# One attention batch moved beside chunk 1's first layer, and both layers of the feed-forward part taken in turn from there on

**Chip, cores, metric.** One core of one Trainium2 chip. The time is device microseconds of an execution; "span" is the length of the profiled execution. "Before" was run again with every group of experiments, on the same chip as these, and its median went from 357.4 to 360.3 us. So kernels are compared by their ratio to the kernel before in the same rounds, not by their microseconds across groups.

## The reference

Sliding-window attention (window of 64 keys) over 8 batches of 8 heads, 576 positions, 64 features; its output feeds two matrix products with `h - tanh(h)` between them.

```python
scores = scale * np.matmul(q, k.transpose(0, 1, 3, 2))
mask = (rel >= 0) & (rel < window)          # rel = row - column, window = 64
attn = softmax(np.where(mask, scores, -1e9))
x = np.matmul(attn, v)                      # -> [4608 tokens, 512]
h = x @ w_in                                # [4608, 2048]   "first layer"
out = (h - np.tanh(h)) @ w_out              # [4608, 512]    "second layer"
```

## The kernel before: what the argument touches

The program is one list of **slots**. A slot holds at most one layer product, of four matmuls of 512 columns. Tokens are in 9 chunks of 512, attention is in 32 head pairs `g` (four per batch, `b = g // 4`). `at(h, fn, ...)` hangs other work on slot `h`; in the traces each engine runs its own instructions in this program order, so a slot is a place in each engine's queue and not a time. PE multiplies matrices, DVE and ACT work on elements, POOL casts and issues loads, SP issues the other transfers (DMA).

```python
NR, NPT = 2, 4                                   # buffers of q/k, of probabilities
v_pool = ctx.enter_context(tc.tile_pool(name="v", bufs=1))
vb = const.tile([PV, EV, H, D + 1], BF16, ...)   # a batch's values, cast: ONE buffer
vw = [const.tile([128, NJ, H, D + 1], BF16, ...) for i in range(2)]   # its 9 windows

def pace(h):             # holds POOL's queue until the last first-layer product before slot h is done
    c, m = [OPS[i][1:] for i in range(h) if OPS.get(i, "-")[0] == "h"][-1]
    nc.gpsimd.tensor_copy(tick, gT[c][0:1, m, 0:1])

# chain of a batch's values: load (POOL's DMA queue) -> cast_v into vb -> windows_v (SP's DMA queue, vb -> vw) -> pv (PE)
# x of a batch (b >= 3): norm (DVE) -> x_dma: transposing DMAs on SP's queue -> first-layer products
...
for m in range(M):                               # M = 16 products per chunk and layer
    OPS[2 * m] = "h", 0, m                       # "h": first layer, "y": second layer
    OPS[32 + m] = "y", 0, m
    OPS[48 + m] = "h", 1, m
    OPS[64 + m] = "y", 1, m
    OPS[80 + m] = "h", 2, m
    for c in range(3, NC):                       # from chunk 3 on both layers in turn
        OPS[32 * c + 2 * m] = "h", c, m
        OPS[32 * c + 2 * m + 1] = "y", c - 1, m
...
at(46, lambda: [cast_v(2, pr, V) for pr in range(NP)])        # V: DVE
at(47, lambda: [windows_v(2, j, Y) for j in range(NJ)])       # Y: SP's queue
# batches 2 and 3: a table of slots per pair, from 48 to 91; batch 3's x_dma at 92
```

The softmax here doesn't subtract the row's maximum and nothing guards it: scores larger than these inputs give would overflow.

## Time and profile before

| | before |
|---|---|
| median of 4 runs | 360.31 us (356.45 to 361.85) |
| span of the profiled run | 358.4 us |
| PE busy | 321.5 us, 90% |
| slot 48 / 64 / 96 starts (us) | 68.8 / 88.6 / 140.5 |

The slot times are read from the trace: PE's layer products stand in it in program order, so the start of the first of each four is the start of its slot. The profile's lines are shown and read in the prediction.

### The profile page before, as it was taken

How to read it: one execution, taken by the hardware profiler on the slowest of the kernel's cores; microseconds unless marked ns; L12 is line 12 of the kernel's file. 1: busy time of each engine (PE TensorE's matmuls, PEld its weight loads, DVE VectorE, ACT ScalarE, POOL GpSimd, SP SyncE). 2: the span in 40 equal slices, each digit the busy share in tenths (PEclk: the TensorE clock that was granted, in tenths of full speed). 3: DMA queues.
4: the chain of work that ended last, by engine and by line, in shares of the span. 5: the costliest groups of instructions: out<-in, count | busy, mean ns of one | idle time of the engine just before them, and what ended most of it. 6: DMA issues, size and time to landing. Idle time of an engine off the chain costs nothing.

```text
span 358.4 us, 6075 instructions
## 1 busy us (share of the span) xinstructions
PE 321.5 (90%) x2346; PEld 177.1 (49%) x2346; DVE 207.2 (58%) x344; ACT 182.9 (51%) x332; POOL 98.4 (27%) x148
## 2 busy tenths in 40 slices
PE   6789998699787986778879999999999999999995
PEld 2554454455454553435445555555555444444442
DVE  4566765677954885346657767665666334433300
ACT  3536545288554764516636566655554444444421
POOL 8821090033731610517063445801000000000000
PEclk9559999699999999969999999999999999999999
DMA  8999999839189206991856989489930410010012
GB/s 162 167 199 215 182 160 207 148 49 183 29 119 247 60 1 118 134 170 45 157 119 112 203 145 174 125 140 202 203 108 29 98 59 29 31 59 29 31 67 79
DMA packets 54653, 42.96 MB, mean 120 GB/s; under 512 B 23232, under 2 KB 48320, under 8 KB 54624
## 3 DMA queue, kind: packets, MB, share of 16 engines
q0 software_dynamic: 20816, 18.73, 34.5%
q1 hardware_dynamic: 33456, 23.42, 28.0%
q10 hardware_dynamic: 352, 0.43, 0.5%
q8 instruction: 18, 0.29, 0.3%
q14 instruction: 11, 0.09, 0.1%
HBM read 36.70 MB, written 11.21 MB: 134 GB/s over the span
## 4 chain that ended last, share of the span: by engine, by line
PE 62%; DMA 17%; DVE 11%; ACT 4%; POOL 3%; issue 2%; POOLq 0%; ACTq 0%
PE ps L417 28%; PE ps L393 26%; DMA vall<-in_v_dram 11%; DMA vw<-vb 5%; DVE gT L405 3%; DVE xs L357 3%; PE ps L346 3%; PE ps L334 3%; DVE qt L86 2%; PE ps L267 2%; DMA qall<-in_q_dram 2%; ACT qt L84 1%; ACT th L398 1%; ACT pt L336 1%; PE ps L363 1%
## 5 line engine op out<-in xcount | busy, mean ns | idle before, releaser
L393 PE MATMUL ps<-xT,wi 128*128 128x512 bf16 x576 | 146.2, 383 | 6.6 <-DVE gT L405 6.5
L417 PE MATMUL ps<-w_out_sb,gT 128*128 128x512 bf16 x576 | 145.7, 382 | 0.5 <-ACT ysb L422 0.5
L405 DVE TENSOR_TENSOR gT<-ps,th 128x512 bf16<-128x512 f32 x144 | 98.3, 690 | 80.8 <-ACT th L398 79.1
L398 ACT ACTIVATE th<-ps 128x512 f32<-128x512 f32 x144 | 85.6, 598 | 85.5 <-PE ps L393 81.4
L393 PEld LDWEIGHTS <-wi 128*128 128x128 bf16 x576 | 62.1, 114 | 55.6 <-issue 9.8
L417 PEld LDWEIGHTS <-gT 128*128 128x128 bf16 x576 | 53.6, 98 | 53.9 <-issue 1.8
L336 ACT ACTIVATE pt<-ps 128x384 bf16<-128x384 f32 x72 | 35.1, 488 | 30.8 <-PE ps L334 30.6
L357 DVE TENSOR_TENSOR xs<-ps,rc 64x576 bf16<-64x576 f32 x48 | 36.2, 755 | 1.2
L422 ACT ACTIVATE ysb<-ps 128x512 f32<-128x512 f32 x36 | 21.5, 596 | 19.1 <-PE ps L417 19.1
L346 PE MATMUL ps<-vw,pt 128*128 128x130 bf16 x216 | 22.3, 220 | 7.7 <-DMA vw<-vb 5.8
L86 POOL COPY vb<-vall 72x1024 bf16<-72x1024 bf16 x20 | 20.9, 1067 | 28.9 <-DMA vall<-in_v_dram 17.8
L346 PEld LDWEIGHTS <-pt 128*128 128x128 bf16 x216 | 16.9, 98 | 19.1 <-issue 6.6
L334 PE MATMUL ps<-qt,kt 128*128 128x128 bf16 x216 | 24.2, 222 | 1.3 <-ACT pt L336 1.2
L334 PEld LDWEIGHTS <-kt 128*128 128x128 bf16 x216 | 17.1, 99 | 14.2 <-issue 5.3
L86 DVE COPY qt<-ps 64x576 bf16<-64x576 bf16 x20 | 15.2, 760 | 13.8 <-ACT qt L84 13.7
L86 POOL COPY qb<-qall 96x768 bf16<-96x768 bf16 x16 | 13.2, 825 | 30.2 <-DMA qall<-in_q_dram 30.2
L340 DVE TENSOR_TENSOR pt<-pt,ps 128x1152 bf16<-128x1152 bf16 x24 | 17.9, 747 | 0.2
L86 POOL COPY kb<-kall 96x768 bf16<-96x768 bf16 x20 | 16.5, 828 | 0.0
L84 ACT ACTIVATE kt<-ps 128x576 bf16<-128x576 bf16 x20 | 13.0, 650 | 4.7 <-PE ps L267 4.6
L353 DVE RECIPROCAL rc<-ps 128x9 f32<-128x9 f32 x24 | 5.2, 215 | 16.8 <-PE ps L346 16.7
L84 ACT ACTIVATE qt<-ps 64x576 bf16<-64x576 bf16 x20 | 12.7, 637 | 3.1 <-PE ps L267 3.1
L309 ACT ACTIVATE pt<-ps 128x640 bf16<-128x640 f32 (+1 forms) x16 | 10.0, 649 | 5.7 <-PE ps L306 5.6
(74 smaller groups left out, 189.0 us busy)
## 6 DMA issues: line engine op xcount, KB each, us to landing
out_dram<-ysb SPq DMA_DIRECT2D x36, 256.0 KB
vw<-vb SPq DMA_DIRECT2D x48, 130.0 KB
vall<-in_v_dram POOLq DMA_DIRECT2D x7, 576.0 KB, 13.7
kall<-in_k_dram POOLq DMA_DIRECT2D x5, 576.0 KB, 7.1
qall<-in_q_dram POOLq DMA_DIRECT2D x5, 576.0 KB, 9.4
wi<-in_moe_w_in_dram POOLq DMA_DIRECT2D x2, 1024.0 KB, 12.8
w_out_sb<-in_moe_w_out_dram POOLq DMA_DIRECT2D x2, 1024.0 KB, 20.9
kall<-in_k_dram POOLq DMA_DIRECT2D x11, 144.0 KB, 13.8
```

The lines of the kernel that those rows point to most:

```text
L84: nc.scalar.activation(o, i, ACT.Copy)
L86: eng.tensor_copy(o, i)
L334: nc.tensor.matmul(sp[:, i, :], kT[g % NR][:, 64 * j:64 * j + 128], qT[g % NR][:, :, 64 * j:64 * j + 64], start=True, stop=True)
L336: nc.scalar.activation(PT[g % NPT][:, 3 * grp:3 * grp + 3, :], sp, ACT.Exp, scale=scale)
L340: nc.vector.tensor_tensor(p, p, mask.unsqueeze(1).to_broadcast([128, 2 * NJ, 64]), ALU.mult)
L346: nc.tensor.matmul(ps[:, 5 + grp, 130 * i:130 * i + 130], PT[g % NPT][:, j, :], vw[b % 2][:, j, 2 * pr:2 * pr + 2, :], start=True, stop=True)
L357: nc.vector.tensor_tensor(xo[r, :, :, pr, :], ov[r, :, :, h, 0:D], rc[r].to_broadcast([64, 3, 3, 64]), ALU.mult)
L393: nc.tensor.matmul(hp, w_in_tile(ki, m), chunk_tile(c)[:, :, ki % 2, 64 * (ki // 2):64 * (ki // 2) + 64], start=(ki == 0), stop=(ki == 3))
L398: nc.scalar.activation(th, hp, ACT.Tanh)
L405: nc.vector.tensor_tensor(gT[c][:, m, :], hp, th, ALU.subtract)
L417: nc.tensor.matmul(yp, gT[c][:, m, s * 128:(s + 1) * 128], w_out_sb[:, m, :], start=(m == 0), stop=(m == M - 1))
L422: nc.scalar.activation(ysb, ps[:, yp_bank(c, s), :], ACT.Copy)
```

## The change

Its intent: first-layer products alone make PE wait for tanh and subtraction, so after chunk 1's first layer both layers alternate. For that, chunk 2's input (batch 2) must be ready by slot 66 and not 80. So batch 2 goes entirely beside chunk 1's first layer (slots 48 to 65), its mask added by a product on PE ahead of the scores, its value products in column tiles; batches 3 to 5 move with it, and batch 3's loads lose the `pace` that held them. Cut to its core (left out: the layers' PSUM banks, batch 6, and the slots of some casts):

```diff
-        OPS[64 + m] = "y", 1, m
-        OPS[80 + m] = "h", 2, m
+        OPS[66 + 2 * m if m < 15 else 95] = "h", 2, m
+        OPS[63 + 2 * m if m > 1 else 64 + m] = "y", 1, m
...
-    at(35, load_v_all, 2)
     for g in 8, 9, 10, 11:
         at(35, load, g, "k", G)
         at(35, load, g, "q", G)
+        if g == 8:
+            at(35, load_v_all, 2)
...
-    at(46, lambda: [cast_v(2, pr, V) for pr in range(NP)])
-    at(47, lambda: [windows_v(2, j, Y) for j in range(NJ)])
-    at(54, pace, 54)
-    at(54, load_all, 3, "k")   # q at 55, v at 56; values cast at 67-70, windows at 71
+    at(47, cast_pair, 8, V)
+    at(48, cast_pair, 9, G)
+    at(49, lambda: [cast_v(2, pr, V) for pr in range(NP)])
+    at(50, lambda: [windows_v(2, j, Y) for j in range(NJ)])
+    at(52, load_all, 3, "k")   # q at 52, v at 53
+    for i, (g, p) in enumerate(((8, 58), (9, 59), (10, 61), (11, 63))):
+        at(48 + 3 * i, tr, g, "q", 3, A, V)
+        at(49 + 3 * i, tr, g, "k", 3, A)
+        for j in range(3):
+            at(50 + 3 * i + j, hidden_scores, g, j, 4 + (3 * i + j) % 2)   # mask product + scores
+        at(p, tile_pv, g, (6, 7))
...
-    LOADS = {4: (77, 78, 79), 5: (97, 98, 99), 6: (128, 130, 113)}      # slots of k, q, v
+    LOADS = {4: (63, 64, 72), 5: (96, 99, 102), 6: (124, 128, 114)}
+        if b == 3:
+            a = (62, 67, 72, 76)[pr]        # a: slot of the pair's first transpose
+            cv, ky = 63 + pr, 67            # cv: slots of the value casts, ky: first windows
-        if b == 4: a = (89, 95, 101, 108)[pr]; cv, ky = 91 + pr, 95
+        elif b == 4: a = (80, 87, 95, 102)[pr]; cv, ky = 77 + 3 * pr, 88
-        elif b == 5: a = 110 + 7 * pr; cv, ky = 108 + pr, 112
+        elif b == 5: cv, ky = 107 + 2 * pr, 114
             at(ky + j // 2, windows_v, b, j, Y)      # unchanged: nine windows over five slots
```

## The prediction

> **What bounds the kernel now.** I read the page first, then the table of busy time in stretches of 10 us, then the waits of PE, then PE's order of instructions from 56 to 220 us, then the DMA packets. The table by stretches tells where there is anything to win:
>
> ```profile
> core 0: us, PE busy (x) PEld busy (x) DVE busy (x) ACT busy (x) POOL busy (x), PEclk, DMA share, GB/s
> ...
> 60.00:70.00 10.00, 5.70 (x101) 4.11 (x100) 6.50 (x16) 4.10 (x9) 0.64 (x1) 0.69 0.92 161
> ...
> 130.00:140.00 10.00, 5.83 (x44) 3.53 (x44) 8.41 (x14) 5.07 (x9) 0.00 (x0) 1.00 0.35 62
> ...
> 150.00:160.00 10.00, 6.03 (x23) 2.73 (x22) 3.72 (x6) 2.46 (x6) 1.59 (x2) 0.66 1.07 191
> ...
> 210.00:220.00 10.00, 10.00 (x78) 5.87 (x77) 7.12 (x12) 6.14 (x13) 5.81 (x9) 1.00 1.01 176
> ```
>
> From 210 us to the end PE is full: there both layers alternate with one head pair of attention per eight slots. All that can be won lies between 60 and 210 us, where PE's busy sums to 125.0 of 150 us. Each stall also hides some 0.17 us (a matmul's record is 0.38 us, its pitch 0.216), so about 40 stalls add 6 to 7 us; two cold stretches (PEclk 0.69 and 0.66) cost about 4. In all about 35 us are lost there, and that is the ceiling. PE's order of instructions names the causes:
>
> ```profile
> 60.74 0.44 PE L306 MATMUL ps<-qs,kt 64*128 64x64 bf16 x18
> 62.34 0.51 PE L322 MATMUL ps<-vw,pt 128*64 128x65 bf16 x20 [1.17 <-ACT pt L309]
> 64.81 1.14 PE L363 MATMUL ps<-ident,xs 128*128 128x128 bf16 x9 [1.96 <-DVE xs L328]
> ...
> 92.92 0.41 PE L267 MATMUL ps<-ident,kb 96*128 96x96 bf16 x6 [1.85 <-DVE qt L86]
> ...
> 140.47 1.02 PE L393 MATMUL ps<-xT,wi 128*128 128x512 bf16 x4 [2.47 <-DVE gT L405]
> ...
> 152.13 0.22 PE L346 MATMUL ps<-vw,pt 128*128 128x130 bf16 x1 [1.94 <-DMA vw<-vb]
> 153.48 0.27 PE L346 MATMUL ps<-vw,pt 128*128 128x130 bf16 x1 [1.14 <-DMA vw<-vb]
> 154.64 0.27 PE L346 MATMUL ps<-vw,pt 128*128 128x130 bf16 x1 [0.89 <-DMA vw<-vb]
> ```
>
> The stall at 64.81 goes back to DVE's own order:
>
> ```profile
> 62.32 1.45 DVE L86 COPY vb<-vall 72x1024 bf16<-72x1024 bf16 x4 [1.65 <-DMA vall<-in_v_dram]
> 63.69 0.20 DVE L326 RECIPROCAL rc<-ps 128x10 f32<-128x10 f32 x1
> ```
>
> DVE stood for the third batch's values (1.65 us), cast them (1.45 us), and only then normalized what PE waited for. The 2.47 us is chunk 2's first layer run alone: each product needs a tanh and a subtraction, and the subtraction stands behind copies in DVE's queue. The 152 to 155 us stall is the value windows of batch 4, queued behind the transposes of x and sharing the DMA engines with the loads of batch 5.
>
> **What the Trainium skill says.** "TensorE: Matmul & The Clock Gate", Part 1 (the HAM clock gate): half clock after some 3.4 us of idling. The trace agrees: after 149-154.6 us eight matmuls of 512 columns took 3.4 us, against 1.73 warm. [...]The two halves of a query copy do run one after the other (ACT 73.03 to 73.68, DVE from 73.80)[...]. "DMA: Bandwidth & Descriptors", Issuing engines are not separate DMA queues: all share the same 16 engines. Agrees: with nothing else running, windows move at 120 packets of 1040 bytes per us (71-74 us), beside batch 5's loads at 25 to 75 (149-152 us). "TensorEngine Tiling (Array Packing)", Key Properties: changing the tiling mode drains the array. No gap is visible here: 20 products in column tiles take 0.51 us at 60.30, the nine full-width ones they replace also 0.51 of pitch.
>
> **The change part by part.** Slots are the program's scale (one layer product of four matmuls each, 0.864 us of pitch); slot 48 starts chunk 1's first layer, slot 96 chunk 3's.
>
> Start of slot 48. The cast of batch 2's values moves from slot 46 to 49, and its load goes behind the ninth pair's. DVE can then normalize at 60.9 in place of 63.69 us; x is transposed once the product of values at 62.34 is out, at 62.85 in place of 64.81. The rest follows 1.9 us earlier: slot 48 at 66.9, before 68.8.
>
> Slots 48 to 63 (chunk 1's first layer with all of batch 2). PE: 16x0.864=13.8; 8 transpose groups x0.26=2.1; 12 score groups x0.17=2.0, plus 12 mask products of 384 columns x0.16=1.9 (added); 4 value products x0.5=2.0; one transposition of x 1.0; cold start 0.8; in sum 23.6. DVE loses 4 maskings x0.75=3.0 and 4x(1.73-1.03)=2.8 in normalizing. With 16x0.63 subtractions it has about 20, ACT about 18: PE bounds, but in-order waits remain. The transposes of q and k now stand in adjacent slots and share bank 3; ACT's half (0.65) and DVE's (0.76) must both finish between: 1.9 us after the first, 0.7 for the next three, and the first three products' tanh chain costs 1 more. About 5. Slot 64 then starts at 95.5, against 88.6 before, with about 6 us more attention done.
>
> Slots 64 to 95. Layer products 32x0.864=27.6; rest of x of batch 2 1.0; batch 3: 2.1+2.0+2.0=6.1; batch 4's part 2.7 (1.7 of it pulled forward). Sum 37.4. The first-layer products now come every second slot with a second-layer one between, so the waits on DVE (5.9 us in the list of PE's waits from 60 to 160 us) should be nearly gone: 1 left. Other small waits 2, batch 3's windows 1.
>
> End of that stretch. x of batch 3 is moved by transposing DMAs at slot 92 as before, and the last window of batch 4 (slot 92 too, registered after it) queues behind them. Before, from the normalization's end (134.94) to the first window behind the transposes took 6.2 us, so about 7.5 to land; its reader is now at slot 95, about 2.1 us after that normalization. Stall 5.4, and cold clock 1.5. Slot 96 at 95.5+37.4+4+6.9=143.8, near the 142.6 of before.
>
> After slot 96. Before: 215.8 us with about 13.5 lost up to 210. Pure work 202.3, less 1.7 done already: 200.6. Batches 4 and 5 have 7 to 8 slots per pair where they had 6 to 7, and the windows of batch 4 are ahead of batch 5's loads (slots 96 to 102), so the 4 us of idling and 2 us of cold at 149-158 go. But batch 5's last window stands at slot 118 right behind the next transposes, and is read at slot 123: about 4, with 1 of cold; other waits 1.5. So 207.1, and a span of about 351; the times run some 0.4% over the span (359.76 to 358.4), so 352. I take 351, as stalls estimated one by one partly overlap.
>
> **The rivals.** (A) The gain stays: the mixed order removes waits on DVE, the window stalls are small because transfers run ahead. For it: 210 us on, where the same mix has no idle time with similar load per slot. Against it: batch 3's pairs stand four to five slots apart there, and the transposes do precede the windows. It would give 338 to 346. (B) The stalls only change place: denser attention in slots 48-63 waits on bank 3, and the windows of batches 4 and 5 stand behind the transposes at slots 92 and 118. For it: 6.2 us from normalization to window as measured, readers five slots after. Against it: those windows are one of nine, the others are ahead. It would give 354 to 360. (C) Batch 3's loads, now issued near 74 us beside batch 2's windows, delay the first value product (slot 58, about 85 us) or batch 3's windows. For it: windows (3) took from 99 to 115 us beside loads. Against it: the uncontended ones landed within 12 us of the first issue, and slot 58 leaves about that. It would add 2 to 5 us to any of the above. My number is between A and B.
>
> **Range and chances.** Two per cent is 352.6. The sum gives 351 to 352; its doubtful terms are the two window stalls (12 together with cold) and bank 3's waits (5), each of which could halve or grow by half: 342 to 358 for 8 in 10. No more than the added mask products (1.9) and denser waits could make it slower, which needs every stall to be larger: 0.03. Faster 0.57, same 0.40.
>
> **What would show each step right or wrong.** In the profile after: slot 48 (12 matmuls of chunk 1's first layer) near 67 us; no wait of DVE for values near 62; waits of the key transposes on the query copy between 68 and 90; chunk 1's first layer ending near 95; few waits of first-layer products on DVE after 97; a stall on a window just before chunk 3 starts and another some 30 us later, both with a lowered PEclk. If those two are under 2 us each, the time will be near 343 and B is wrong. If PE's busy from 60 to 210 us is no larger than 125 plus 3, the reasoning on the mixed order is wrong. If batch 2's value products wait for windows, C is right.

## The result

379.66 us (median of 4, 377.81 to 380.37), against 360.31. The ratio is 1.0567, with an interval of 1.047 to 1.0664: **slower by over 5%**. Ratios and intervals are those from the fast runs of the same rounds; they are not quite the ratios of the medians. The prediction (351, range 342 to 358, "slower" at 0.03) was wrong.

The waits of PE changed their kind. First the list of PE's waits before, then after (columns: the waiting instruction, what ended the wait, us in total, times, longest):

```profile
PE ps L393 <- DVE gT L405: 6.5, 8, 2.5
PE ps L346 <- DMA vw<-vb: 5.8, 6, 1.9
```

```profile
PE ps L346 <- DMA vw<-vb: 14.4, 7, 3.8
PE ps L322 <- DMA vw<-vb: 3.7, 4, 1.8
PE ps L334 <- DMA kt<-kd: 3.7, 2, 2.9
...
PE ps L393 <- DVE gT L405: 0.8, 2, 0.5
```

What the change was made for happened: first-layer products (L393) wait for DVE's subtraction 0.8 us in all, where they waited 6.5. In its place value products (L346, L322) wait 18.1 us for their windows, where they waited 5.8. PE's order of instructions after shows those waits, batch by batch:

```profile
85.69 0.22 PE L322 MATMUL ps<-vw,pt 128*64 128x65 bf16 x2 [0.27 <-DMA vw<-vb]
87.74 0.22 PE L322 MATMUL ps<-vw,pt 128*64 128x65 bf16 x2 [1.83 <-DMA vw<-vb]
88.62 0.22 PE L322 MATMUL ps<-vw,pt 128*64 128x65 bf16 x2 [0.66 <-DMA vw<-vb]
89.75 0.32 PE L322 MATMUL ps<-vw,pt 128*64 128x65 bf16 x4 [0.90 <-DMA vw<-vb]
...
91.10 1.91 PE L393 MATMUL ps<-xT,wi 128*128 128x512 bf16 x4
...
122.72 0.22 PE L346 MATMUL ps<-vw,pt 128*128 128x130 bf16 x1 [2.99 <-DMA vw<-vb]
...
156.81 0.22 PE L346 MATMUL ps<-vw,pt 128*128 128x130 bf16 x1 [3.77 <-DMA vw<-vb]
...
189.55 0.22 PE L346 MATMUL ps<-vw,pt 128*128 128x130 bf16 x1 [1.69 <-DMA vw<-vb]
191.71 0.27 PE L346 MATMUL ps<-vw,pt 128*128 128x130 bf16 x1 [1.94 <-DMA vw<-vb]
...
198.36 0.27 PE L346 MATMUL ps<-vw,pt 128*128 128x130 bf16 x1 [2.73 <-DMA vw<-vb]
```

After each group of waits four matmuls take 1.7 to 1.9 us in place of 1.03 (here at 91.10): the granted clock is half, here from 89.1 to 95.9 us, after 156.81 from 157.3 to 160.7. That costs 1.7 us more, so the stall of 3.8 us cost some 5.5.

The slot times give the balance, and beside it what the prediction said:

| stretch | before | after | difference | predicted length |
|---|---|---|---|---|
| start to slot 48 | 68.8 | 65.4 | -3.4 | 66.9 |
| slots 48 to 63 | 19.8 | 37.1 | +17.2 | 28.6 |
| slots 64 to 95 | 51.9 | 54.7 | +2.8 | 48.3 |
| slot 96 to the end | 217.9 | 220.5 | +2.6 | 207.1 |
| span | 358.4 | 377.6 | +19.2 | 351 |

The first stretch came better than predicted. DVE no longer stands for batch 2's values near 62 us. The other three missed by 8.5, 6.4 and 13.4 us.

**Why the windows come late.** The trace after shows the reasons batch by batch. For batch 2, DVE casts the values late (behind a query copy that waits 3.17 us for ACT's half), slowly (2.97 us, the first two beside POOL's copies), and SP can only then issue the windows:

```profile
69.40 0.76 DVE L86 COPY qt<-ps 64x576 bf16<-64x576 bf16 x1 [3.17 <-ACT qt L84]
70.19 0.69 DVE L405 TENSOR_TENSOR gT<-ps,th 128x512 bf16<-128x512 f32 x1
70.80 2.97 DVE L86 COPY vb<-vall 72x1024 bf16<-72x1024 bf16 x4
```

```profile
73.84 0.63 SPq L176 DMA_DIRECT2D vw<-vb  x1
74.56 6.34 SPq L161 DMA_DIRECT2D vw<-vb  x8
```

At the same moment (72.4 to 75.0 us) POOL issues batch 3's three loads, with no `pace` ahead of them any more. In the record of DMA packets no packet moves from 66.0 to 73.9 us, although the values had landed by 61; then loads and windows share the engines until 89.7 us. The first packet of a window moves 4.1 us after its issue (77.9), behind loads; in e8 below, without them, 1.3 us after.

For batch 3, three of the four value casts stand in POOL's queue behind the paced load of batch 4, which waits for a first-layer product that PE is late with:

```profile
90.12 1.05 POOL L86 COPY vb<-vall 72x1024 bf16<-72x1024 bf16 x1 [4.19 <-PE ps L322]
91.10 0.83 POOL L86 COPY qb<-qall 96x768 bf16<-96x768 bf16 x1
102.42 0.18 POOL L452 COPY tick<-gT 1x1 bf16<-1x1 bf16 x1 [10.49 <-DVE gT L405]
102.66 0.77 POOL L103 DMA_DIRECT2D kall<-in_k_dram  x1
103.43 1.06 POOL L86 COPY vb<-vall 72x1024 bf16<-72x1024 bf16 x1
```

For batches 4 and 5 the ninth window stands behind the transposes of x, as predicted. Batch 4's:

```profile
149.70 2.93 SPq L378 DMA_TRANSPOSE xT<-xs  x2
153.16 0.60 SPq L161 DMA_DIRECT2D vw<-vb  x1
```

### The profile page after: what moved, and what is told of

Read it like the earlier page. It is cut to its first block, busy times and chain, and to the rows that moved or that the text cites. A ratio compares the mean times of both kernels' runs of the same rounds, so it can differ in the third digit from the quotient of the medians.

```text
span 377.6 us, 6190 instructions
## 1 busy us (share of the span) xinstructions
PE 330.6 (88%) x2402; PEld 178.9 (47%) x2402; DVE 199.5 (53%) x330; ACT 183.9 (49%) x332; POOL 103.5 (27%) x153
## 4 chain that ended last, share of the span: by engine, by line
PE 61%; DMA 20%; DVE 7%; POOL 4%; ACT 4%; issue 2%; SPq 1%; POOLq 0%; ACTq 0%; DVEq 0%
PE ps L417 26%; PE ps L393 26%; DMA vw<-vb 9%; DMA vall<-in_v_dram 7%; PE ps L334 3%; PE ps L346 2%; PE ps L267 2%; DVE gT L405 2%; DMA qall<-in_q_dram 2%; DMA kt<-kd 1%; DMA kall<-in_k_dram 1%; DVE qt L86 1%; DVE xs L357 1%; DVE vb L86 1%; ACT th L398 1%
## 5 line engine op out<-in xcount | busy, mean ns | idle before, releaser
L393 PE MATMUL ps<-xT,wi 128*128 128x512 bf16 x576 | 151.8, 392 | 1.1 <-DVE gT L405 0.8
L393 PEld LDWEIGHTS <-wi 128*128 128x128 bf16 x576 | 62.2, 115 | 48.8 <-issue 5.4
L336 ACT ACTIVATE pt<-ps 128x384 bf16<-128x384 f32 x60 | 29.4, 490 | 47.0 <-PE ps L334 47.0
L346 PE MATMUL ps<-vw,pt 128*128 128x130 bf16 x180 | 21.4, 223 | 16.6 <-DMA vw<-vb 14.4
L357 DVE TENSOR_TENSOR xs<-ps,rc 64x576 bf16<-64x576 f32 x40 | 30.2, 755 | 1.0
L346 PEld LDWEIGHTS <-pt 128*128 128x128 bf16 x180 | 15.0, 99 | 23.5 <-issue 6.6
L334 PE MATMUL ps<-qt,kt 128*128 128x128 bf16 x180 | 20.8, 227 | 5.4 <-DMA kt<-kd 3.7
L86 POOL COPY kb<-kall 96x768 bf16<-96x768 bf16 x23 | 19.2, 837 | 13.3 <-ACT pt L309 6.0
L334 PEld LDWEIGHTS <-kt 128*128 128x128 bf16 x180 | 14.2, 101 | 18.0 <-issue 8.8
L86 POOL COPY qb<-qall 96x768 bf16<-96x768 bf16 x19 | 15.9, 839 | 14.8 <-PE ps L267 9.4
L452 POOL COPY tick<-gT 1x1 bf16<-1x1 bf16 x12 | 2.2, 180 | 47.7 <-DVE gT L405 47.7
L340 DVE TENSOR_TENSOR pt<-pt,ps 128x1152 bf16<-128x1152 bf16 x20 | 14.9, 746 | 0.1
```

Source lines behind the costliest of these rows:

```text
L86: eng.tensor_copy(o, i)
L334: nc.tensor.matmul(sp[:, i, :], kT[g % NR][:, 64 * j:64 * j + 128], qT[g % NR][:, :, 64 * j:64 * j + 64], start=True, stop=True)
L336: nc.scalar.activation(PT[g % NPT][:, 3 * grp:3 * grp + 3, :], sp, ACT.Exp, scale=scale)
L340: nc.vector.tensor_tensor(p, p, mask.unsqueeze(1).to_broadcast([128, 2 * NJ, 64]), ALU.mult)
L346: nc.tensor.matmul(ps[:, 5 + grp, 130 * i:130 * i + 130], PT[g % NPT][:, j, :], vw[b % 2][:, j, 2 * pr:2 * pr + 2, :], start=True, stop=True)
L357: nc.vector.tensor_tensor(xo[r, :, :, pr, :], ov[r, :, :, h, 0:D], rc[r].to_broadcast([64, 3, 3, 64]), ALU.mult)
```

## Experiments

Theory W: nearly all of the loss is transfers in unlucky slots (late casts, loads beside windows, a window behind transposes). Rival D: the denser attention beside chunk 1's first layer costs by itself (bank 3, DVE and ACT in order). All kernels gave right results, except where it is said. Slot times of an experiment are its own; stretches are compared, as starts differ by 1 to 2 us.

### e1: batch 2's values and windows earlier

```diff
-    at(49, cast values 2 on DVE); at(50, windows 2)
+    at(47, cast values 2 on DVE); at(47, windows 2)      # ahead of cast_pair(8)
```

> Edit: the casts of batch 2's values go from slot 49 back to the end of slot 47 (ahead of the eighth pair's casts, behind the last copies of x), and its windows are issued there too. Theory W (value windows land late because they are issued late and beside a batch's loads): the casts run near 65.6-67.1 us at 0.36 us each (they took 0.74 each beside POOL's casts), the windows land by about 77 us, the stall at the first value product of batch 2 (3.7 us at 85-89.7 us, then some 3 us of half clock) is gone, slot 64 comes at about 96 in place of 102.4 us and the time falls by 3 to 7 us, to 373-377. Rival D (the denser attention beside chunk 1's first layer is itself what costs: bank 3, DVE and ACT in order): slot 64 moves by under 1.5 us.

375.70 us median beside 358.25 for before. Two of its four runs took 370.54 and 373.82. No ratio was given, so the time settles nothing. The trace does: no value product of batch 2 waits for a window, the four casts took 1.42 us, and slots 58 to 62 took 7.4 us against 13.9. Slots 48 to 58 took 2.0 us longer (20.7 against 18.8), with a colder clock at their start and the query copy behind the casts. The stall is what W said; of the 6 us expected by slot 64 (reckoned from slot 48) 4.5 came in this order.

### e2: batch 3's values cast ahead of the paced load

```diff
-            cv, ky = 63 + pr, 67
+            cv, ky = 62, 67
```

> Edit: POOL casts batch 3's values at slot 62, all four ahead of the paced load of batch 4 (slot 63), where three of them stood behind it. POOL waited 10.5 us at that pace with the values landed. Theory W: the casts end near 94 us in place of 108, the windows of batch 3 start near 95 in place of 108.2, meet idle DMA engines (no packet moved from 92 to 104 us), and the stall of 4.3 us at 119.7-124.5 us with its cold clock is gone: 4 to 6 us less at slot 80, time 373-376 if later stalls stay. Rival D: windows start early but slot 80 moves by under 2 us, since PE would wait on DVE or ACT there.

Ratio 1.0448 (1.0362 to 1.0534), against 1.0567. POOL's four casts now run together, and windows start at 97.3 us in place of 108.2:

```profile
93.24 4.03 POOL L86 COPY vb<-vall 72x1024 bf16<-72x1024 bf16 x4 [4.26 <-DMA vall<-in_v_dram]
97.20 0.84 POOL L86 COPY qb<-qall 96x768 bf16<-96x768 bf16 x1
104.48 0.18 POOL L452 COPY tick<-gT 1x1 bf16<-1x1 bf16 x1 [6.44 <-DVE gT L405]
```

The wait on batch 3's windows is gone; slots 76 to 80 took 4.9 us against 11.9. As W expected, and against D. Of these 7.0 us the whole time keeps some 4 (1.2%).

### e3: the ninth window ahead of the transposes

```diff
-                at(ky + j // 2, windows_v, b, j, Y)
+                at(ky + min(j // 2, 3), windows_v, b, j, Y)
```

> Edit: the ninth window of every batch from 3 on is issued one slot earlier, so that for batches 4 and 5 it stands ahead of the transposes of x instead of behind them. Theory W as the prediction had it (rival B): the stall of 3.8 us before chunk 3 (152.9-156.8 us) and the one of 2.7 us at 195.6-198.4 us go, with some 1.5 us of cold clock each; 6 to 9 us less, 371-374. If the transposes themselves then come later and first-layer products of chunk 3 wait for x, under 4 us are won.

Ratio 1.0431 (1.0356 to 1.0506). The stall before chunk 3 is gone, and x of batch 3, now next in the queue, makes the first product of chunk 3 wait only 0.6 us:

```profile
153.62 0.63 PE L346 MATMUL ps<-vw,pt 128*128 128x130 bf16 x3
155.10 1.05 PE L393 MATMUL ps<-xT,wi 128*128 128x512 bf16 x4 [0.60 <-DMA xT<-xs]
```

Slots 94 to 98 took 6.0 us against 10.3, slots 120 to 124 10.6 against 13.5. The sum, 7.2 us, is in the range expected; the whole time fell by less, some 5 us (1.4%). At slot 120 other windows of batch 5 stay late.

### e4: the change without the mixed order

```diff
-        OPS[66 + 2 * m if m < 15 else 95] = "h", 2, m
-        OPS[63 + 2 * m if m > 1 else 64 + m] = "y", 1, m
+        OPS[64 + m] = "y", 1, m
+        OPS[80 + m] = "h", 2, m            # and the banks of before
```

> Edit: all of the change but the mixed order: chunk 1's second layer (slots 64 to 79) and chunk 2's first (80 to 95) run one after the other again, with the banks of before. If the mixed order gains as the slot times say (from slot 64 to 76 the changed kernel makes up 4.9 us on the one before), this is 3 to 6 us slower than the changed kernel: 382-386. If the mixed order is what costs, it is faster than the changed kernel by over 3 us. Theory W expects the window stalls to remain in either, so at least 375.

Ratio 1.0596 (1.0508 to 1.0684), as slow as the changed kernel: the difference expected did not show, in either direction. From slot 62 to 80, with second-layer products alone and batch 3's windows late as well, it took 28.9 us against 31.1; from 80 to 96, with first-layer products alone, 30.5 against 28.0, where five of them waited 5.3 us for DVE. So the order has the effect that it was made for, but between these window stalls its net worth in the whole chunk is nil. Whether it is worth something without them is e9's question.

### e5: the three repairs together

> Edit: the three earlier edits together (batch 2's values and windows at slot 47, now behind the casts of pair 8; batch 3's values cast ahead of the paced load; ninth windows one slot earlier). Theory W: the gains add, since they sit in different stretches: against the kernel before on the same chip, the changed kernel was 1.057, the single edits 1.043 to 1.049, so together about 1.057-0.01-0.012-0.013=1.02, 365-368 us where before has 358-360. If they do not add (one stall only waits for the next transfer), over 1.035.

(The edits of e1 to e3; in e1's the casts now stand behind those of pair 8.) Ratio **1.0065** (0.9988 to 1.0142). So three placements, which touch no arithmetic, bring back 5.0 of the 5.7% (the changed kernel's ratio is from its own rounds). e2 and e3 alone gave 1.2 and 1.4; e1 has no ratio of its own.

### e6: transfers of batches 4 and 5 in the idle stretch

```diff
-    LOADS = {4: (63, 64, 72), 5: (96, 99, 102), ...
+    LOADS = {4: (63, 64, 67), 5: (80, 81, 82), ...
-  b == 4: cv, ky = 77 + 3 * pr, 88      b == 5: cv, ky = 107 + 2 * pr, 114
+  b == 4: cv, ky = 72 + pr, 76          b == 5: cv, ky = 93 + pr, 104
```

(on top of e5; batch 5's loads no longer wait for x of batch 3)

> Edit: the three, and the transfers of batches 4 and 5 moved into the stretch where no packet moves (126-142 us in the changed kernel): batch 4's values loaded at slot 67, cast at 72-75, windows at 76; batch 5's loads at 80-82, values cast at 93-96, windows at 104. Theory W: the remaining waits on windows (about 6 us around 184-191 us, with cold clock) go, and slots 92 to 124 take about 35 us: a ratio of 0.98 to 1.0 to before. If PE then waits for x of batch 3 or for windows of batch 4 beside these loads: over 1.01.

Ratio 0.9967 (0.9906 to 1.0028), at the upper part of the range expected. PE's waits on windows are down to 1.7 us in one wait (batch 3's, at 116.3 us); x of batch 3 makes PE wait 1.6. Slots 92 to 124 took 38.8 us, not 35. Three rows of the table of stretches, 60 to 210 us, of the kernel before, the changed one and e6 (columns as in the prediction's: PE, PEld, DVE, ACT, POOL busy, PE's clock, share and rate of DMA):

```profile
60.00:210.00 150.00, 124.99 (x1010) 73.73 (x1009) 98.86 (x162) 85.05 (x164) 54.26 (x74) 0.95 0.67 119
```

```profile
60.00:210.00 150.00, 119.23 (x957) 67.36 (x957) 80.99 (x131) 75.58 (x145) 51.70 (x70) 0.91 0.60 105
```

```profile
60.00:210.00 150.00, 130.88 (x1136) 77.02 (x1150) 97.53 (x160) 91.89 (x174) 60.49 (x80) 1.00 0.75 131
```

The changed kernel does not have too much work in this stretch but too little: PE, DVE, ACT, POOL and the DMA engines are all less busy than before. That is what a kernel looks like that waits for the order of its transfers. In e6 all but DVE are busier than before and the clock is whole.

### e7: the mask on DVE again (on top of e6)

```diff
-            at(50 + 3 * i + j, hidden_scores, g, j, 4 + (3 * i + j) % 2)
+            at(50 + 3 * i + j, scores, g, j, 4 + (3 * i + j) % 2)
+        at(53 + 3 * i, masking, g)
```

> Edit: the one before it, with batch 2's mask as a DVE product after the exponential, as before the change, in place of the twelve mask products on PE. PE is relieved of 12x0.16=1.9 us and of their waits, DVE gets 4x0.75=3.0 us. If PE bounds that stretch, 1 to 2 us faster than the run before it; if DVE's order is what PE waits for there, the same or up to 2 us slower.

Ratio 0.9965 (0.9897 to 1.0033), the same as e6. From slot 48 to 96 it takes 3.0 us longer than e6 (80.3 against 77.3). It has 0.9 of this back from before slot 48 and 2.2 from after slot 144, where its wait for keys is 1.9 us against 2.6 and its clock stays whole (e6's is half from 243.3 to 246.7). So in this stretch the mask product on PE looks like the better choice by up to 3 us, though the times do not show it: it costs PE 1.9 us but spares DVE's queue, where PE then waits 1.8 us for the mask (once) and more for query copies.

### e8: only batch 3's loads held back

```diff
-    at(52, load_all, 3, "k"); at(52, load_all, 3, "q"); at(53, load_v_all, 3)
+    at(57, pace, 57); at(57, load_all, 3, "k"); at(57, load_all, 3, "q"); at(57, load_v_all, 3)
```

> Edit: the changed kernel, with batch 3's three loads held from slots 52-53 to slot 57 and nothing else. The windows of batch 2, issued at the same time as before (from 73.8 us), then have the DMA engines alone. If sharing is why they come late: the stall of 3.7 us at 85-89.7 us is gone or under 1 us, though batch 3 then comes some 10 us later and waits turn up at slots 62 to 75; the time may not change. If it is their late issue alone, the stall stays over 2.5 us.

The stall on batch 2's windows falls from 3.7 us to one wait of 0.23:

```profile
87.55 0.25 PE L322 MATMUL ps<-vw,pt 128*64 128x65 bf16 x4 [0.23 <-DMA vw<-vb]
```

Slots 48 to 63 took 31.9 us, against 37.1. So sharing the engines with the loads is enough to explain that stall, with the issue as late as it was (9.2 us after the start of slot 48, 8.5 in the changed kernel). e1 shows that an earlier issue removes it too: either suffices. The ratio is 1.0434 (1.0342 to 1.0526), but one of the four runs was slow, and value products waited 15.8 us for windows of later batches.

### e9: the repaired kernel in phases

> Edit: the kernel with its transfers mended (e6_gap, 0.997 of before), with the two layers one after the other again as in e4_phases. With the window waits gone nothing hides the order's own worth. If the mixed order gains what the prediction said (waits of first-layer products on DVE, about 5 us), this is 3 to 6 us slower than e6_gap: a ratio of 1.005 to 1.015. If it gains nothing, within 1 us of e6_gap.

(e4's edit on e6.) Ratio 1.0081 (0.9993 to 1.0169) against e6's 0.9967, in different groups, and the intervals overlap. From slot 48 to 144 it took 133.5 us, e6 129.8. Not all of these 3.7 us belong to the order:

```profile
PE ps L346 <- DMA vw<-vb: 4.0, 4, 2.0
PE ps L393 <- DVE gT L405: 4.0, 4, 3.0
```

The waits on windows are batch 3's (the first, 1.3 us, just before slot 76, the others in slots 76 to 80), with the clock half from 111.9 to 118.8 us; e6 has one wait of 1.7 us there and a whole clock. These four slots took 2.5 us longer than in e6, while slots 48 to 76 took 1.2 us less. The order shows in slots 80 to 96: there first-layer products wait for DVE's subtraction (in e6 under 0.4 us, but 1.6 for x), and the stretch took 2.4 us longer. So by these two executions the mixed order is worth some 1 us at most (2.4 less 1.2), and the rest is late windows again. No pair of runs compares the two orders with the windows out of the way in both.

### e10: batch 7's windows earlier (on top of e6)

```diff
+        elif b == 7: cv, ky = 152 + 2 * pr, 159
```

> Edit: e6_gap with batch 7's values cast at slots 152 to 158 and its windows at 159 (before 163 and 166 on), so that they leave the queue of the bounced keys free. Theory W in its late form: the wait for transposed keys near slot 185 (2.6 us in e6_gap, 3.7 in the changed kernel) with its cold clock goes, 3 us less: a ratio of 0.987 to 0.992. If keys are late for another reason (POOL's wait on the bounce), the wait stays.

A failure: ratio 1.0134 (1.0051 to 1.0216). The wait for transposed keys fell from 2.6 to 1.6 us, but a new one for batch 6's last keys came, which POOL casts behind batch 7's first query copy:

```profile
PE ps L267 <- POOL kb L86: 4.5, 1, 4.5
PE ps L334 <- DMA kt<-kd: 1.6, 1, 1.6
...
224.77 0.95 POOL L122 COPY qz<-qall 96x384 bf16<-96x384 bf16 x2 [13.24 <-DMA qall<-in_q_dram]
```

(The last line is from POOL's order.) The queries landed 16.8 us after their issue, 8.1 in e6: here their packets moved at the same time as those of the transposes of x. A second wait of 3.1 us for POOL, at 119 us, lies before anything that the edit touches (e6's there is 0.9).

### e11 and e12: the kernel before, with the change's load order, then also batch 4's windows earlier

```diff
 e11:  the diff's move of load_v_all(2), and
-    at(46, cast values 2 on DVE)
+    at(47, cast values 2 on DVE)           # behind the copies of x
 e12:  e11 and
-            cv, ky = 91 + pr, 95           # batch 4
+            cv, ky = 83 + pr, 86
```

> Edit: the kernel before, with only the first part of the change: batch 2's values loaded behind pair 8's queries and keys, and cast at slot 47 behind the copies of x rather than at slot 46. The change's slot 48 came 3.4 us earlier than before (65.35 against 68.77). If that comes from this, slot 48 is near 66 us and 1.5 to 3.5 us are won, unless a later wait takes them back; ratio 0.990 to 0.998.

> Edit: the run before it, and batch 4's values cast at slots 83 to 86 and its windows issued from slot 86, ahead of the transposes of x at slot 92, where they stood behind them (slot 95). The stall of before at 149.2-154.6 us (4 us of waits on windows, some 2 us of cold clock) should go: 5 to 7 us less than the run before it, a ratio of 0.972 to 0.985. If PE then waits elsewhere for DVE in that stretch, under 3 us.

e11: ratio 1.0031 (0.9966 to 1.0096), no gain. Slots 44 to 48 took 12.0 us, against 14.6 before, so the step itself works. But slot 44 came 3.7 us late in this execution, and by slot 100 the kernel was within 1 us of before, where batch 4's windows stop both. (In e12 and e13, which contain this edit, slot 48 starts at 66.7 and 66.0.)

e12 gave a **wrong result** (relative error 0.31) by a fault of mine: windows 0 and 1 were issued in slot 86, and the last pair's cast hangs on the same slot but was registered after them, so they carried old values. SP issues them at 121.52 us, the cast runs at 126.14. Its time (0.9952) is told for completeness; it also shows a wait for x of 5.6 us, as the windows kept SP until 133 us.

### e13: the kernel before, batch 4's values loaded, cast and windowed earlier

```diff
-    LOADS = {4: (77, 78, 79), ...        cv, ky = 91 + pr, 95
+    LOADS = {4: (77, 78, 74), ...        cv, ky = 80 + pr, 84     # on top of e11
```

> Mends e12, whose windows 0 and 1 were issued in the slot in which the last pair's values were cast, ahead of that cast, so that they carried old values. Edit to e11 (the kernel before with the change's load order): batch 4's values loaded at slot 74, cast at 80-83, windows from 84. The stall on windows of before at 149-154.6 us should go, and with the windows out of the way the transposes at slot 92 go at once, so no wait for x as in e12 (5.6 us): 5 to 7 us less than before, a ratio of 0.980 to 0.988. If x or batch 5's keys are late instead, about 0.995 as e12.

Ratio **0.9855** (0.9776 to 0.9935), 352.39 us beside 358.41: the lowest ratio of all, with no new order of the layers at all. The gain is under 2%, and the interval overlaps that of e14 below. Slots 96 to 124 took 36.7 us, 43.3 before. PE's waits on windows are down from 5.8 to 0.4 us. What stays on top of its list is the wait that the change was made against:

```profile
PE ps L393 <- DVE gT L405: 5.9, 7, 2.5
PE ps L267 <- DVE qt L86: 5.4, 5, 2.2
```

### e14 and e15: e6 with batch 7's keys and queries loaded earlier, then also the mask on DVE

```diff
-    LOADS = {..., 6: (124, 128, 114)}
+    LOADS = {..., 6: (124, 128, 114), 7: (146, 147, 142)}
```

> Edit to e6_gap (0.997): batch 7's keys and queries loaded at slots 146 and 147, ahead of the first cast of its values (slot 148), where POOL held the queries' load back by 6.3 us waiting for those values. Theory: the bounced keys are late near slot 185 because the bounce starts late; the wait of 2.6 us and its cold clock go: 3 us less, a ratio of 0.985 to 0.992. If SP's queue of windows is what holds the keys, the wait stays.

> Edit to e14: batch 2's mask on DVE instead of PE, as in e7. In e6 and e7 the two came out alike (0.9967 and 0.9965), with e7 0.8 us ahead only because its wait for keys was smaller; so within 1 us of e14, or slower by up to 2 us by slot 96, where e7 was 2 us behind.

e14: ratio 0.9907 (0.984 to 0.9973). Faster than before, but by the lower half of what was expected: the wait for keys is 2.0 us in two, not gone. e15: 0.9949 (0.9885 to 1.0013), not told apart from e14 by time; from slot 48 to 96 it takes 2.4 us longer, as e7 took 3.0. Why keys still come late there stays open. SP's queue, in which bounced keys and windows stand in one order, is a candidate that no run settles.

## Why the prediction was wrong

The term that failed is the stalls on windows. The sum had 10.4 us of waits for them (1, 5.4 and 4) and 2.5 us of cold clock. Measured are 18.1 us of waits, and by an estimate from the clock's record some 12 more (half of the 23.9 us at half clock that begin in or after these waits): 30 us in place of 13, that is 17 of the 26.6 us between 351 and the span of 377.6. Point by point, by its own steps:

1. **Start of slot 48: right.** Predicted 66.9 us, measured 65.4; no wait of DVE for values near 62. The 1.5 us beyond it are luck: e2, e3, e4 and e8, which are the same program up to here, have 66.1 to 67.6.
2. **The mixed order: right in mechanism, too large in worth.** Waits of first-layer products on DVE were to fall from 5.9 to 1 us; in the trace they fell from 6.5 to 0.8. But second-layer products now wait 1.3 us for the subtraction, and e9 against e6 leaves some 1 us for the order as a whole. The prediction's own test of this step, PE busy for over 128 of the 150 us from 60 to 210, failed (119.2), though for the window stalls: in e6 it is 130.9.
3. **Slots 48 to 63: the failing step.** Without the window stall this stretch takes 29.3 us (e5 and e6), against 28.6 predicted, so PE's work and bank 3's waits were well sized in total. Of the other 7.7 us, 6.4 lie in slots 58 to 63: batch 2's windows with the cold clock after them, for which the sum had nothing. The other 1.3 come earlier and fit a half clock from 72.0 to 75.4 us, which e5 and e6 do not have. The prediction named this as rival C, and even quoted the number that decides it: windows (3) took from 99 to 115 us beside loads. Then it argued with the 12 us that windows take alone. Measured: issued at 73.8, in time by its reckoning (85 less 12), and moved only by 89.3, 15.5 us later (before, beside loads, 97.8 to 114.6). Where the new schedule puts a load beside the windows, the duration to use is the one measured beside a load. e8 settles it: without the loads the stall is gone.
4. **Slots 64 to 95: "batch 3's windows 1", mis-sized.** It was 4.3 us of waiting and some 3 of cold clock (half from 123.2 to 130.0 us). The packet times were thought of, POOL's order was not: three casts stood behind a `pace` that waits for PE. With the repairs the stretch takes 46.9 us (e5), against 48.3 predicted with 6.9 for the stall at its end. So what remains is 5.5 us over the other 41.4 of the sum, 3.0 of them waits for windows and x that e5 still has; the larger stalls of batches 3 and 4 added the other 8.
5. **Ninth windows of batches 4 and 5 behind the transposes: right**, and e3 shows it. The stall before slot 96 was 3.8 us (5.4 predicted, the clock's 1.5 beside it). At slots 120 to 124 it was 6.4 us of waits and cold clock after each: 13.5 us against 4.9 in e6, so 8.5 lost where 5 were foreseen, because batch 5's other windows were late as well.
6. **After slot 96: pure work "200.6" was some 3 to 5 us too little.** e14 takes 207.5 us there with 2 us of waits for keys. 2.1 us of it is a misreading: the 215.8 us of before run from 142.6, which is the start of slot 98; slot 96 starts at 140.5. The rest may be in the 13.5 us that I subtracted as losses of the kernel before. And the wait for keys near slot 185 (3.7 us, with cold clock) had no term at all.
7. **"No more than the added mask products (1.9) and denser waits could make it slower"**, with 0.03 for it, was the worst sentence. It took the list of PE's waits before for the list of what can go wrong, and forgot its own rivals: B with C on top is 356 to 365 us. A changed schedule makes new waits, and one after another: batch 3's casts stood behind a load that waited for PE, which batch 2's windows had made late.
8. **The gain itself.** Even with its transfers repaired the changed kernel is 0.9% faster than before (e14), not the 2% and more of 351 us. There slots 64 to 95 take 48.4 us and the rest from slot 96 207.5, with no large window stall in them; the prediction had the same totals (48.3 and 207.1) with 6.9 and 5 us of stalls inside. So its sums of work were up to 12 us too small; some 4 of this are a wait of 2.1 us for POOL and a half clock from 118.8 to 122.2 us in that execution.

Two slips of reading changed little: windows alone move at 116 to 156 packets per us from 71 to 74 us, not 120, and beside loads at 38 to 104 (149 to 152), not 25 to 75; and 2% under the median of 360.31 is 353.1, not 352.6.

Shown by experiment: the placements cost 5.0% together (e5), each removes the stall it was aimed at (e1, e2, e3), taking the loads away suffices for batch 2's (e8), and the mixed order is masked by them (e4). Rival D is refuted as the cause of the loss: with the same dense attention e5 stands at 1.0065, its interval around 1. Not shown: what the mixed order is worth alone (some 1 us by e9 and e6, with late windows in e9), and why the keys of batch 7 are late.

## What to carry to other kernels

When work is moved earlier in a hand-made schedule, walk its inputs back through every in-order queue (load, cast, copy, consumer) and check what stands ahead of each in its own queue, above all waits that were harmless while the consumer was later. Time each transfer with the duration measured beside the transfers it will really share the engines with. And before reordering the arithmetic, try to repair the transfers in the kernel as it is: here that alone (e13) gave the lowest ratio, 0.9855, against 0.9907 for the changed order with its transfers repaired (e14), and the two intervals overlap.

## What the Trainium skill lacked or had wrong

- "DMA: Bandwidth & Descriptors", Issuing engines are not separate DMA queues: says that all queues interleave on the same 16 engines, which the trace bears out. What such a mix costs does not stand in that section. Here nine windows of 130 KB took 11 us from the first issue to the last packet alone or nearly so (63.8 to 75.1 in the kernel before, 76.1 to 87.0 in e8), and 15.5 to 17 beside a batch's loads (73.8 to 89.3 and, before, 97.8 to 114.6 us).
- "SBUF — State Buffer", Who interferes with whom: states that a copy on VectorE in its 2-port mode and a GpSimd instruction block each other fully. Nothing is lacking here; the trace fits it, though no run shows in which mode DVE's casts ran: the two casts of values beside POOL's copies took 1.00 and 1.04 us, each of the four in e1, without POOL, 0.42. (The third, beside a DMA issue of POOL's, took 0.76, the fourth, beside the next, 0.41.) It would have predicted one part of batch 2's delay, had I looked there.
- "TensorEngine Tiling (Array Packing)", Key Properties: says that a change of tiling mode drains the array, without a duration. My "no gap is visible" was wrong (59.34+0.864 against 60.30 us before; after the change too): value products in column tiles start 0.10 us after the pitch of the products ahead of them ends (97.21 against 96.25+0.864 us), where a transposition at 98.85 follows with none.
- "TensorE: Matmul & The Clock Gate", Part 1: half clock after a window of idling; its subsection on PSUM-queue cycling adds frequent short idles, but not how much of them it takes. Here waits of 0.27 to 1.83 us, 3.7 us in all from 85.4 to 89.8 with small products between, were enough: the clock was half from 89.1 to 95.9 us, and four matmuls took 1.91 us in place of 1.03 at 91.10.
